# A mixer kernel on one NeuronCore: raw halves of the next pair kept, sums from PSUM copies, GpSimd forming most blocks

## The chip, the cores and the metric

The kernel runs on one core of a Trainium2 chip. What counts is the device time of one execution in microseconds (us). Five engines work at the same time, each through its own instructions in order: TensorE (PE, matrix products; its weight loads are shown as PEld), VectorE (DVE), ScalarE (ACT), GpSimd (POOL) and SyncE (SP, which here only issues DMA transfers). They wait for each other through semaphores. SBUF is the working memory, PSUM the eight banks that TensorE writes its products to, HBM the main memory. GpSimd works on SBUF alone in this kernel.

## The reference

Inputs are float32. Eight batches of 576 tokens pass a windowed attention (8 heads of 64), and then a mixer:

```python
scores = scale * np.matmul(q, k.transpose(0, 1, 3, 2))
mask = (rel >= 0) & (rel < window)
scores = np.where(mask, scores, -1000000000.0)
attn = np.exp(scores - max); attn = attn / (sum + 1e-09)
x = np.matmul(attn, v)                      # 8 x 576 x 512
h = np.maximum(xt @ w_tok1, 0.0) @ w_tok2   # over the tokens, 576 -> 256 -> 576
u = x + h.transpose(0, 2, 1)
h2 = np.maximum(u @ w_ch1, 0.0) @ w_ch2     # over the channels, 512 -> 1536 -> 512
return (u + h2).astype(np.float32)
```

The change concerns the last product over the channels alone. The 8 x 576 tokens are 4,608 columns there.

## The kernel before

**Precision.** Every float32 operand of a large product is kept as two tiles: a high one, a rounded copy that ScalarE makes, and a low one, the difference between the value and its high part. Three matmuls (high x high, low x high, high x low) stand for one product.

**Stages.** Attention and the products over the tokens fill the first 253 us and leave `u` in HBM, as nine chunks of 512 columns (`u_dram`). Then come the channel products. Chunk 0 is done plainly. Chunks 2 and 1 are the *half pair*: the first layer is plain, the second is done on both chunks together with seven products in place of eight (the scheme of Strassen and Winograd on 2 x 2 blocks). Chunks 3 and 4, 5 and 6, 7 and 8 are *pairs*, with seven products in both layers. The seven are called m1 to m7 and run in the order m1, m6, m5, m7, m3, m2, m4 in a pair's first layer.

**The blocks of a pair.** A pair's first layer needs seven combinations of its `u`. With four raw tiles r11, r12, r22, r21 (128 x 512, one quarter of the pair; there are two such sets, t = 0 and t = 1, and the text calls them halves) they are t1 = r12 - r11, r12' = r22 - r12, t2 = r22 - t1 (`sums`, lines 867 to 872) and r11' = r21 - t2 (`sum4`, line 876). `prep` (lines 880 to 888) then forms one half of a block: ScalarE's copy is the high part (line 886), a subtraction on VectorE or GpSimd the low part (line 888). m1 is formed from r11, m6 from t2, m5 from t1, m7 from r12', m3 from r22, m2 from r21, m4 from r11'. r11 and r12 are overwritten by their sums, so m1 has to be formed before `sum4`.

**The half pair's second layer** runs in three groups. Each group has two `mixed_product` calls (first layer, 24 matmuls each) and two `second_product` calls, one for each `ct`. A second product has seven products of six matmuls; each product lands in one of four PSUM banks P, Q, R, S (m1 and m2 share P, m7 and m4 share R, m5 and m3 share S, m6 has Q), and VectorE adds the bank to the output (line 1082) before the next product may use it. After m6, three sums follow: one on VectorE into c22, two on GpSimd into c12 and c21. In the last group the order is m7, m1, m5, m6, m2, m3, m4 for ct = 0 and m7, m5, m1, m6, m3, m2, m4 for ct = 1. The banks of ct = 1 for R and S are the two buffers of the tag `h`.

**What is woven in.** The order on each engine is written by hand: after each product `second_product` calls `after(m)`, and the functions `after0`, `after1`, `tail0` and `tail1` put the work for the first pair's blocks there. In the middle group the raw tiles of half 0 are loaded, GpSimd forms their sums, and m1 and m6 of half 0 are formed. Then half 1 is loaded into the same four tiles, and later half 0 a second time into four other tiles (`homes`), because its raw tiles are gone. In the last group `tail0` forms sums and blocks of half 1, `tail1` those of half 0, both sums on VectorE. m2 and m4 come last, since the tiles that they lie in hold the half pair's weights until its last product.

**After it** `first_product` of the first pair follows on TensorE at once. Its products m1, m6, m5, m7 start the banks P, Q, S, R; VectorE forms x1 (line 1037) from Q and a ScalarE copy of P (line 1034), and x2 (line 1040) from S. m3 adds to S, so it has to wait until x2 has read S.

**Loads.** SyncE issues all of them, in program order. `load_unit` brings the pairs' weights in pieces, two transfers of 896 KB each.

Of the kernel before, what the change touches and what calls it, by code (L numbers as in the profile page):

```python
# [11 lines left out]
F32 = mybir.dt.float32  # L12
# [11 lines left out]
P = 128  # L24
# [71 lines left out]
def mixer_kernel(ctx: ExitStack, tc: tile.TileContext, qh, kh, vh, wt1, wt2, wc1, wc2, out):  # L96
# [493 lines left out]
    with ExitStack() as bctx:  # L590
# [195 lines left out]
        def ended(steps):  # L786
            assert next(steps, None) is None
# [62 lines left out]
        pairs = [(j, j + 1) for j in range(N_PLAIN + N_MIXED, NCHUNK, 2)]  # L850
        comb, raws, pools = {}, {}, {}

        def load_raw(q, t, at=0, homes={}):
            r = raws[at] = {}

            def new(name):
                if name in homes:
                    return homes[name]
                return pools[at].tile([P, CHUNK], F32, name=f"{name}_{q}_{t}", tag=name, bufs=1)

            for name, j, ct in (("r11", 0, t), ("r12", 1, t), ("r22", 1, 2 + t), ("r21", 0, 2 + t)):
                r[name] = new(name)
                nc.sync.dma_start(r[name], u_dram[pairs[q][j]][:, ct])
            for name in ("t1", "t2"):
                r[name] = new(name)

        def sums(t3=True, at=0, eng=nc.vector):
            r = raws[at]
# [131 lines left out]
        def first_product(n, q, f, after, earlier):  # L1000
# [24 lines left out]
            for k, m in enumerate(PRODUCTS):  # L1025
                o = n % NSLOT * SLOT + k * 2 * P
                c = comb[q, m]
                for z, t in enumerate((1, 0) if q == 0 and m in ("m5", "m7", "m3") else (0, 1)):
                    at = slice(o + t * P, o + (t + 1) * P)
                    for y, (w, h) in enumerate(((w1hi, 0), (w1hi, 1), (w1lo, 0))):  # L1030
                        nc.tensor.matmul(b[INTO[m]], w[:, at], c[:, h, t], start=(k < 4 and z == y == 0),  # L1031
                                         stop=(z == 1 and y == 2), skip_group_check=True)
                if m == "m1":
                    nc.scalar.copy(x1, pp)  # L1034
                    next(earlier, None)
                elif m == "m6":
                    nc.vector.tensor_add(x1, qq, x1)
                    next(earlier, None)
                elif m == "m5":
                    nc.vector.tensor_add(x2, ss, x1)  # L1040
                    next(earlier, None)
                elif m == "m7":
                    nc.vector.tensor_add(qq, rr, x2)
                    raw_block("m3", qq)
                elif m == "m3":
                    nc.vector.tensor_add(ss, ss, x1)
                    nc.scalar.activation(g12, ss, AF.Relu)
                    raw_low("m3", qq)
                    positive(t3, qq, g12)
                    sum_block("m7", t3)  # L1050
                elif m == "m2":
                    positive(t1, pp, g12)
                    sum_block("m5", t1)
                    nc.vector.scalar_tensor_tensor(out=t2, in0=qq, scalar=0.0, in1=t1, op0=ALU.max, op1=ALU.add)
                    raw_block("m1", pp)
                    sum_block("m6", t2)
                    raw_low("m1", pp)
                after(m)
# [67 lines left out]
        for g in range(NG):  # L1126
# [14 lines left out]
                    prep(0, {"m3": "m1", "m2": "m6"}[m], 0)  # L1141

            def tail0(m):
                if m == "m6":
                    sums()
                if m in ("m2", "m3"):
                    prep(0, {"m2": "m5", "m3": "m7"}[m], 1, 0, nc.gpsimd)
                if m in ("m3", "m4"):
                    prep(0, {"m3": "m1", "m4": "m6"}[m], 1)
                if m == "m4":  # L1150
                    sum4()

            def tail1(m):
                if m == "m7":
                    prep(0, "m3", 1, 0, nc.gpsimd)
                if m == "m6":
                    sums(True, 1)
                if m in ("m3", "m2", "m4"):
                    prep(0, {"m3": "m5", "m2": "m7", "m4": "m3"}[m], 0, 1, nc.gpsimd)
                if m == "m4":  # L1160
                    sum4(1)

            odd = (3 * g + 1) % 2
            tags = BANKS[odd]
            for i in range(2):
# [3 lines left out]
                if last and i == 0:  # L1169
                    ended(steps)  # L1170
                if last and i == 1:
                    load_unit(0)
                    homes = {name: pg.tile([P, CHUNK], F32, name=f"{name}_x", tag=tag, bufs=1)
                             for name, tag in (("r11", "g12"), ("r12", "t1g"), ("r22", "t2g"), ("r21", "t3g"))}
                    spare = new_tmps(pm, "wt").rearrange("p (n a) c -> p n (a c)", a=2)
                    homes |= {"t1": spare[:, 0], "t2": spare[:, 1]}
                    load_raw(0, 0, 1, homes)
                    load_unit(1)
                    load_unit(2)
            for ct in range(2):  # L1180
                second_product(-1, g, ct, (odd + 1 + ct) % 2, (*slots[ct], 0), (u2c[0], u1[0]), u2[ct],
                               ((after0, after1), (tail0, tail1))[last][ct])
                if g == 1 and ct == 1:
                    load_raw(0, 1)
                load_mixed(2 * g + 2 + ct)
                if not last:
                    store_quarters(2)
        for m, eng in (("m2", nc.vector), ("m4", nc.gpsimd)):
            for t in range(2):
                prep(0, m, t, 1 - t, eng)  # L1190
        mctx.close()
        pools[1] = bctx.enter_context(tc.tile_pool(name="pg2", bufs=1, reuse_waits="tile"))

# [93 lines left out]
```

## Time and profile before

| what | value |
|---|---|
| runs of the kernel | 796.96, 797.24 and 798.72 us, median 797.24 |
| the profiled execution | 798.98 us, of which 797.2 us are the profile's span |
| PE busy | 781.1 us (98%), 5,713 matmul instructions |
| DVE busy | 596.2 us (75%) |
| ACT busy | 403.1 us (51%) |
| POOL busy | 342.3 us (43%) |
| last group of the half pair, ct = 0 | from 420.49 us |
| ct = 1 | from 430.01 us |
| first product of the first pair | from 442.47 us |
| second product of the first pair | from 468.08 us |

Times are from the start of the span. "Busy" counts the time in which an engine had an instruction under way. TensorE's matmuls overlap, so that a matmul of 0.39 us is followed by the next after 0.227 us. A row of the timeline gives start, duration, engine, line, operation, what is written and read, and in brackets the idle time before it with what ended it. A row of the waits gives who waited for whom, and then the total in us, the number of waits and the longest. The granted clock (PEclk) is the share of TensorE's full clock. A tile's name is given without its buffer number: `r` is a raw tile of the first set of four, `r_x` one of the second set, `m` a block, `uf` an output tile, `u_x` the sum that m1 and m6 share, `x` is x1 or x2, `gp` and `op` are PSUM banks of the first and second layer.

### The profile page before, as it was taken

To read this page: it belongs to the slowest core of one execution; us is meant where nothing else is said; L and a number is where in the kernel's file an instruction comes from. 1 tells how busy PE (TensorE), PEld (TensorE's weight loads), DVE (VectorE), ACT (ScalarE), POOL (GpSimd) and SP (SyncE) were. 2 spreads that over 40 slices of the span, in tenths; PEclk is the share of its full clock that TensorE was granted. 3 is DMA by queue.
4 is the path that set the end of the run, shared out by engine and by line. 5 is a ranking of instruction groups with operands and counts; after the bars stand their busy time and mean duration, and the time that the engine had idled before them with its cause. 6 is when DMAs were issued, how large, how long until landed. Compare 5 with 4: busy or idle time off the path is not lost.

```text
span 797.2 us, 15920 instructions
## 1 busy us (share of the span) xinstructions
PE 781.1 (98%) x5713; PEld 650.0 (82%) x5713; DVE 596.2 (75%) x1550; ACT 403.1 (51%) x1149; POOL 342.3 (43%) x298
## 2 busy tenths in 40 slices
PE   8999999999999999999998899999999999999997
PEld 6778888888888888888887688888888888888886
DVE  6998889689884897768888874757766667656576
ACT  6999979989964432463432342325322244324040
POOL 3654445445430001045667540549732638723140
PEclk9999999999999999999999899999999999999999
DMA  9876768767847569895979375765985756955543
GB/s 343 307 235 228 242 221 303 260 212 267 279 138 244 191 207 284 274 298 175 304 229 408 131 290 191 263 239 197 296 322 195 291 184 207 350 211 192 198 163 106
DMA packets 89552, 192.81 MB, mean 242 GB/s; under 512 B 9088, under 2 KB 52864, under 8 KB 87552
## 3 DMA queue, kind: packets, MB, share of 16 engines
q1 hardware_dynamic: 87360, 189.95, 68.9%
q10 hardware_dynamic: 2112, 1.84, 0.7%
q8 instruction: 45, 0.74, 0.4%
q14 instruction: 35, 0.29, 0.1%
HBM read 149.29 MB, written 42.47 MB: 241 GB/s over the span
## 4 chain that ended last, share of the span: by engine, by line
PE 64%; DVE 2%; DMA 2%; issue 1%; ACT 1%; POOL 0%; DVEq 0%; ACTq 0%; POOLq 0%
PE op L1093 22%; PE gp L1031 21%; PE gp L667 12%; PE op L675 4%; DMA u_dram<-u 1%; DMA out<-uf 1%; DVE uf L1082 0%; PE op-1_0_1_3_5769 L1093 0%; PE op-1_1_1_2_6045 L1093 0%; PE op-1_1_1_0_6043 L1093 0%; PE op-1_1_1_3_6046 L1093 0%; PE op-1_0_1_2_5768 L1093 0%; PE op-1_0_0_2_5691 L1093 0%; PE op-1_0_0_3_5692 L1093 0%; PE op-1_0_0_0_5689 L1093 0%
## 5 line engine op out<-in xcount | busy, mean ns | idle before, releaser
L1031 PE MATMUL gp<-m,w1hi 128*128 128x512 f32 x504 | 157.4, 394 | 3.6 <-DVE x L1040 3.6
L1031 PEld LDWEIGHTS gp<-m,w1hi 128*128 128x128 f32 x504 | 95.9, 190 | 24.1 <-DVE x L1040 4.0
L319 ACT ACTIVATE e<-e,nm 128x128 f32<-128x128 f32 x288 | 112.3, 398 | 5.7 <-DVE nm L311 5.6
L1031 PE MATMUL gp<-m,w1lo 128*128 128x512 f32 x252 | 99.0, 393 | 0.0
L1082 DVE TENSOR_TENSOR uf<-op,uf 128x512 f32<-128x512 f32 (+1 forms) x91 | 61.9, 684 | 39.6 <-PE op L1093 31.8
L117 POOL TENSOR_TENSOR m7lo<-t3g,m7hi 128x512 fp32r<-128x512 f32 x18 | 23.4, 1302 | 148.6 <-ACT m7hi L114 148.6
L311 DVE CUSTOM_DVE_ANT_0 e<-s,mask 128x128 f32<-128x128 f32 x288 | 63.5, 286 | 10.4 <-PE s L292 10.4
L232 POOL TENSOR_TENSOR w<-r,c 128x384 f32<-128x384 f32 (+1 forms) x31 | 30.8, 994 | 67.0 <-DVE r L230 56.0
L667 PE MATMUL gp<-ulo,w1hi 128*128 128x512 f32 x144 | 56.1, 390 | 0.2 <-DVE ulo L117 0.2
L319 ACT ACTIVATION_READ_ACCUMULATOR e<-e,nm 128x1 f32 x288 | 56.4, 196 | 0.0
L667 PE MATMUL gp<-uhi,w1hi 128*128 128x512 f32 x144 | 56.1, 390 | 0.0
L1031 PEld LDWEIGHTS gp<-m,w1lo 128*128 128x128 f32 x252 | 47.9, 190 | 10.1
L667 PE MATMUL gp<-uhi,w1lo 128*128 128x512 f32 x144 | 56.0, 389 | 0.0
L117 POOL TENSOR_TENSOR xlo<-x,xhi 128x512 fp32r<-128x512 f32 x32 | 41.1, 1285 | 29.0 <-ACT xhi L114 28.7
L1034 ACT COPY x<-gp 128x512 f32<-128x512 f32 x18 | 10.6, 588 | 75.8 <-PE gp L1031 75.8
L338 PEld LDWEIGHTS xp<-v,pt 128*64 128x64 f32 x1152 | 36.7, 137 | 13.5 <-ACT e L319 9.0
L437 PE MATMUL up<-t2hi,hhi 128*128 128x320 f32 (+1 forms) x128 | 42.9, 335 | 0.0
L326 PE MATMUL pp<-ident,e 128*128 128x128 f32 x288 | 41.5, 278 | 1.4 <-ACT e L319 0.8
L338 PE MATMUL xp<-v,pt 128*64 128x64 f32 x1152 | 41.7, 225 | 1.1 <-ACT pt L328 0.8
L292 PE MATMUL s<-k,q 64*64 64x128 f32 x1152 | 41.6, 278 | 0.9 <-DVE ri L350 0.5
L328 ACT COPY pt<-pp 128x512 f32<-128x512 f32 x72 | 39.0, 587 | 2.4 <-PE pp L326 0.7
L326 PEld LDWEIGHTS pp<-ident,e 128*128 128x128 f32 x288 | 33.1, 141 | 6.7 <-ACT e L319 5.5
(477 smaller groups left out, 2158.7 us busy)
## 6 DMA issues: line engine op xcount, KB each, us to landing
v<-vh SPq DMA_DIRECT2D x36, 512.0 KB, 4.3
w1hi<-w1s SPq DMA_DIRECT2D x18, 896.0 KB, 5.1
w1lo<-w1s SPq DMA_DIRECT2D x18, 896.0 KB, 7.0
w1hi<-w2s SPq DMA_DIRECT2D x18, 896.0 KB, 4.7
w1lo<-w2s SPq DMA_DIRECT2D x18, 896.0 KB, 6.5
raw<-wc SPq DMA_DIRECT2D x32, 384.0 KB, 5.2
q<-qh SPq DMA_DIRECT2D x36, 256.0 KB, 5.0
k<-kh SPq DMA_DIRECT2D x7, 1280.0 KB, 8.3
```

The lines of the kernel that those rows point to most:

```text
L117: eng_lo.tensor_sub(lo, src, hi.bitcast(F32))
L292: nc.tensor.matmul(so, qt[r, j, half], kbs[b][r, n:n + 2, j], start=True, stop=True)
L311: nc.vector.tensor_tensor_reduce(out=e_sb[i, u][:, h], in0=s_ps[i][h // 2 * 2 + u][:, h], in1=mk, scale=-scale, scalar=MAX_F32, op0=ALU.ad ...
L319: nc.scalar.activation(e[:, h], e[:, h], AF.Exp, bias=nm[:, g:g + 1], scale=-1.0, accum_out=sm[:, g:g + 1])
L326: nc.tensor.transpose(pp[:, h], e[:, h], ident)
L328: nc.scalar.copy(pt, pp)
L338: nc.tensor.matmul(xp[half * BLK:(half + 1) * BLK, h], pts[h % 2][:, h // 2, half * BLK:(half + 1) * BLK], vt[:, half, h], start=True, sto ...
L437: nc.tensor.matmul(up[:, :n], hx[:, cs], w[:, tt * S + s0:tt * S + s0 + n], start=False, stop=(k == 6), skip_group_check=True)
L667: nc.tensor.matmul(gp, w[:, w1_at(ft, ct)], x[:, ct], start=(k == 0), stop=(k == 3 * NCT - 1))
L1031: nc.tensor.matmul(b[INTO[m]], w[:, at], c[:, h, t], start=(k < 4 and z == y == 0), stop=(z == 1 and y == 2), skip_group_check=True)
L1082: eng.tensor_add(x, y, x)
L1093: nc.tensor.matmul(bank[:, cols], w[:, o:o + P], x[:, cols], start=(i == 0 and y == 0 and m in ("m1", "m6", "m7", "m5")), stop=(i == 1 and ...
```

## The change

- The raw tiles of half 0, loaded in the middle group, stay in place to the end. The second set of four tiles is loaded with half 1, and the load of half 1 into the first set is gone: four transfers of 256 KB fewer. r11, r12 and r22 of half 1 now come ahead of the first weight piece, r21 behind it.
- The sums of half 1 are formed by `sums_by_psum`: ScalarE copies r12 and r22 into the two buffers of `h` in PSUM, and each of the three subtractions on VectorE takes one operand from there. VectorE forms no sums of half 0 any more, since those of the middle group are kept.
- `tail0` now forms the low parts of m7, m3 and m5 of half 0 on GpSimd, `tail1` those of m1 and m6 of half 1 on VectorE and of m5, m7 and m3 of half 1 on GpSimd. Both `sum4` come at the end of `tail1`.
- In the first pair's first layer, half 0 comes first for all seven products; before, half 1 came first for m5, m7 and m3.

```diff
+        def sums_by_psum(at):
+            r = raws[at]
+            p12, p22 = (ps.tile([P, CHUNK], F32, name=f"{name}_p", tag=tag, bufs=bufs)
+                        for name, (tag, bufs) in zip(("r12", "r22"), BANKS[1][2:]))
+            nc.scalar.copy(p12, r["r12"])
+            nc.scalar.copy(p22, r["r22"])
+            nc.vector.tensor_sub(r["t1"], p12, r["r11"])
+            nc.vector.tensor_sub(r["r12"], r["r22"], p12)
+            nc.vector.tensor_sub(r["t2"], p22, r["t1"])
...
-                for z, t in enumerate((1, 0) if q == 0 and m in ("m5", "m7", "m3") else (0, 1)):
+                for z, t in enumerate((0, 1)):
...
             def tail0(m):
+                if m in ("m7", "m1", "m5"):
+                    prep(0, {"m7": "m7", "m1": "m3", "m5": "m5"}[m], 0, 0, nc.gpsimd)
                 if m == "m6":
-                    sums()
-                if m in ("m2", "m3"):
-                    prep(0, {"m2": "m5", "m3": "m7"}[m], 1, 0, nc.gpsimd)
-                if m in ("m3", "m4"):
-                    prep(0, {"m3": "m1", "m4": "m6"}[m], 1)
+                    sums_by_psum(1)
+
+            def tail1(m):
+                if m in ("m7", "m5"):
+                    prep(0, {"m7": "m1", "m5": "m6"}[m], 1, 1)
+                if m in ("m1", "m6", "m3"):
+                    prep(0, {"m1": "m5", "m6": "m7", "m3": "m3"}[m], 1, 1, nc.gpsimd)
                 if m == "m4":
-                    sum4()
-
-            def tail1(m):
-                if m == "m7":
-                    prep(0, "m3", 1, 0, nc.gpsimd)
-                if m == "m6":
-                    sums(True, 1)
-                if m in ("m3", "m2", "m4"):
-                    prep(0, {"m3": "m5", "m2": "m7", "m4": "m3"}[m], 0, 1, nc.gpsimd)
-                if m == "m4":
-                    sum4(1)
+                    for t in range(2):
+                        sum4(t)
...
                 if last and i == 1:
-                    load_unit(0)
...
-                    load_raw(0, 0, 1, homes)
+                    loads = raw_loads(0, 1, 1, homes)
+                    next(loads)
+                    load_unit(0)
+                    ended(loads)
                     load_unit(1)
                     load_unit(2)
...
-                if g == 1 and ct == 1:
-                    load_raw(0, 1)
...
         for m, eng in (("m2", nc.vector), ("m4", nc.gpsimd)):
             for t in range(2):
-                prep(0, m, t, 1 - t, eng)
+                prep(0, m, t, t, eng)
```

`raw_loads` is the old `load_raw` as a generator that pauses ahead of r21.

**VectorE, from the c22 sum of ct = 0 on.** In the names, `r12_0_1` is r12 of half 1 in the first set of tiles, `r12_x` a tile of the second set, `r12_p` and `r22_p` the PSUM copies, `wt_wt` the tiles of t1 and t2 in the second set, `op-1_2_0_*` and `op-1_2_1_*` the banks of ct = 0 and ct = 1 (0 is P, 1 Q, 2 R, 3 S), `m1_0` the block m1. Before:

```order
L1082 TENSOR_TENSOR uf1_4745<-u2_x_0_5583,uf1_4745 128x512
L869 TENSOR_TENSOR t1_0_1_6140<-r12_0_1_6134,r11_0_1_6132 128x512
L871 TENSOR_TENSOR r12_0_1_6134<-r22_0_1_6136,r12_0_1_6134 128x512
L872 TENSOR_TENSOR t2_0_1_6141<-r22_0_1_6136,t1_0_1_6140 128x512
L1082 TENSOR_TENSOR uf2_5314<-op-1_2_0_0_6267,uf2_5314 128x512
L1082 TENSOR_TENSOR uf1_4745<-op-1_2_0_3_6270,uf1_4745 128x512
L888 TENSOR_TENSOR m1_0_6095<-r11_0_1_6132,m1_0_6095 128x512
L1082 TENSOR_TENSOR uf2_5314<-op-1_2_0_2_6269,uf2_5314 128x512
L888 TENSOR_TENSOR m6_0_6122<-t2_0_1_6141,m6_0_6122 128x512
L876 TENSOR_TENSOR r11_0_1_6132<-r21_0_1_6138,t2_0_1_6141 128x512
L1082 TENSOR_TENSOR uf1_4745<-op-1_2_1_2_6343,uf1_4745 128x512
L1082 TENSOR_TENSOR uf1_4745<-op-1_2_1_3_6344,uf1_4745 128x512
```

And with the change:

```order
L1098 TENSOR_TENSOR uf1_4745<-u2_x_0_5583,uf1_4745 128x512
L879 TENSOR_TENSOR wt_wt_6246<-r12_p_6302,r11_x_6242 128x512
L880 TENSOR_TENSOR r12_x_6243<-r22_x_6244,r12_p_6302 128x512
L881 TENSOR_TENSOR wt_wt_6246<-r22_p_6303,wt_wt_6246 128x512
L1098 TENSOR_TENSOR uf2_5314<-op-1_2_0_0_6257,uf2_5314 128x512
L1098 TENSOR_TENSOR uf1_4745<-op-1_2_0_3_6260,uf1_4745 128x512
L1098 TENSOR_TENSOR uf2_5314<-op-1_2_0_2_6259,uf2_5314 128x512
L1098 TENSOR_TENSOR uf1_4745<-op-1_2_1_2_6335,uf1_4745 128x512
L904 TENSOR_TENSOR m1_0_6095<-r11_x_6242,m1_0_6095 128x512
L1098 TENSOR_TENSOR uf1_4745<-op-1_2_1_3_6336,uf1_4745 128x512
```

Between the c22 sum and the addition of m5 of ct = 1 (the last row of each) stand ten instructions before and eight with the change; six of the ten read SBUF alone, one of the eight does.

**VectorE, behind the last products of ct = 1.** `x1_0_0` and `x2_0_0` are x1 and x2 of the first pair. Before:

```order
L1082 TENSOR_TENSOR uf1_4745<-u2_x_1_5584,uf1_4745 128x512
L869 TENSOR_TENSOR wt_wt_6258<-r12_x_6255,r11_x_6254 128x512
L871 TENSOR_TENSOR r12_x_6255<-r22_x_6256,r12_x_6255 128x512
L872 TENSOR_TENSOR wt_wt_6258<-r22_x_6256,wt_wt_6258 128x512
L1082 TENSOR_TENSOR uf1_4745<-op-1_2_1_3_6344,uf1_4745 128x512
L1082 TENSOR_TENSOR uf2_5314<-op-1_2_1_0_6341,uf2_5314 128x512
L1082 TENSOR_TENSOR uf2_5314<-op-1_2_1_2_6343,uf2_5314 128x512
L876 TENSOR_TENSOR r11_x_6254<-r21_x_6257,wt_wt_6258 128x512
L888 TENSOR_TENSOR m2_0_6414<-r21_x_6257,m2_0_6414 128x512
L888 TENSOR_TENSOR m2_0_6414<-r21_0_1_6138,m2_0_6414 128x512
L1037 TENSOR_TENSOR x1_0_0_6448<-gp0_0_1_6431,x1_0_0_6448 128x512
L1040 TENSOR_TENSOR x2_0_0_6449<-gp0_0_3_6433,x1_0_0_6448 128x512
```

And with the change:

```order
L1098 TENSOR_TENSOR uf1_4745<-u2_x_1_5584,uf1_4745 128x512
L1098 TENSOR_TENSOR uf1_4745<-op-1_2_1_3_6336,uf1_4745 128x512
L1098 TENSOR_TENSOR uf2_5314<-op-1_2_1_0_6333,uf2_5314 128x512
L1098 TENSOR_TENSOR uf2_5314<-op-1_2_1_2_6335,uf2_5314 128x512
L892 TENSOR_TENSOR r11_0_0_5915<-r21_0_0_5921,t2_0_0_5924 128x512
L892 TENSOR_TENSOR r11_x_6242<-r21_x_6245,wt_wt_6246 128x512
L904 TENSOR_TENSOR m2_0_6405<-r21_0_0_5921,m2_0_6405 128x512
L904 TENSOR_TENSOR m2_0_6405<-r21_x_6245,m2_0_6405 128x512
L1053 TENSOR_TENSOR x1_0_0_6439<-gp0_0_1_6422,x1_0_0_6439 128x512
L1056 TENSOR_TENSOR x2_0_0_6440<-gp0_0_3_6424,x1_0_0_6439 128x512
```

The three sums are gone from here; both `sum4` stand behind the last addition of ct = 1, where one of them stood.

**GpSimd, from the half pair's last first-layer block on.** Before:

```order
L117 TENSOR_TENSOR m4lo_x_5_6211<-g1_2_5248,m4hi_x_5_6210 128x512
L1082 TENSOR_TENSOR uf1_4745<-u2_x_0_5583,uf1_4745 128x512
L1082 TENSOR_TENSOR uf2_5314<-u2_x_0_5583,uf2_5314 128x512
L888 TENSOR_TENSOR m5_0_6314<-t1_0_1_6140,m5_0_6314 128x512
L888 TENSOR_TENSOR m7_0_6325<-r12_0_1_6134,m7_0_6325 128x512
L888 TENSOR_TENSOR m3_0_6352<-r22_0_1_6136,m3_0_6352 128x512
L1082 TENSOR_TENSOR uf1_4745<-u2_x_1_5584,uf1_4745 128x512
L1082 TENSOR_TENSOR uf2_5314<-u2_x_1_5584,uf2_5314 128x512
L888 TENSOR_TENSOR m5_0_6314<-wt_wt_6258,m5_0_6314 128x512
L888 TENSOR_TENSOR m7_0_6325<-r12_x_6255,m7_0_6325 128x512
L888 TENSOR_TENSOR m3_0_6352<-r22_x_6256,m3_0_6352 128x512
L888 TENSOR_TENSOR m4_0_6419<-r11_x_6254,m4_0_6419 128x512
```

And with the change:

```order
L117 TENSOR_TENSOR m4lo_x_5_6201<-g1_2_5248,m4hi_x_5_6200 128x512
L904 TENSOR_TENSOR m7_0_6268<-r12_0_0_5917,m7_0_6268 128x512
L904 TENSOR_TENSOR m3_0_6278<-r22_0_0_5919,m3_0_6278 128x512
L904 TENSOR_TENSOR m5_0_6288<-t1_0_0_5923,m5_0_6288 128x512
L1098 TENSOR_TENSOR uf1_4745<-u2_x_0_5583,uf1_4745 128x512
L1098 TENSOR_TENSOR uf2_5314<-u2_x_0_5583,uf2_5314 128x512
L904 TENSOR_TENSOR m5_0_6288<-wt_wt_6246,m5_0_6288 128x512
L1098 TENSOR_TENSOR uf1_4745<-u2_x_1_5584,uf1_4745 128x512
L1098 TENSOR_TENSOR uf2_5314<-u2_x_1_5584,uf2_5314 128x512
L904 TENSOR_TENSOR m7_0_6268<-r12_x_6243,m7_0_6268 128x512
L904 TENSOR_TENSOR m3_0_6278<-r22_x_6244,m3_0_6278 128x512
L904 TENSOR_TENSOR m4_0_6410<-r11_0_0_5915,m4_0_6410 128x512
```

The same number of instructions; three low parts now stand ahead of the two c12 and c21 sums of ct = 0, one between the two pairs of sums, and two (m7 and m3) behind those of ct = 1.

More of the change, by code (lines that the diff above doesn't have):

```diff
@@ L851, in mixer_kernel, with raw_loads @@
         comb, raws, pools = {}, {}, {}
-        def load_raw(q, t, at=0, homes={}):
+        def raw_loads(q, t, at=0, homes={}):
             r = raws[at] = {}
@@ L861, in load_raw @@
             for name, j, ct in (("r11", 0, t), ("r12", 1, t), ("r22", 1, 2 + t), ("r21", 0, 2 + t)):
+                if name == "r21":
+                    yield
                 r[name] = new(name)
@@ L865, in load_raw @@
                 r[name] = new(name)
+        def load_raw(*args):
+            for _ in raw_loads(*args):
+                pass
+        def sums_by_psum(at):
[7 more added lines that the diff above has]
+            nc.vector.tensor_sub(r["t2"], p22, r["t1"])
         def sums(t3=True, at=0, eng=nc.vector):
```

## The prediction

> **What bounds the kernel now.** I read the chain that ended last first, then TensorE's waits.
>
> ```profile
> PE 64%; DVE 2%; DMA 2%; issue 1%; ACT 1%; POOL 0%; DVEq 0%; ACTq 0%; POOLq 0%
> ...
> 451.64 16.60 PE gp L1031 x60
> 468.24 19.11 PE op L1093 x84
> ...
> 773.84 19.24 PE op L1093 x87
> ```
>
> ```profile
> PE gp L1031 <- DVE x L1040: 3.6, 1, 3.6
> PE op-1_2_1_3_6344 L1093 <- DVE uf L1082: 2.6, 1, 2.6
> PE idle L499 <- DVE zero L166: 1.2, 1, 1.2
> ```
>
> From 451.64 us on the chain is TensorE without a gap, so what is won or lost ahead of that moves the end by as much. TensorE's two longest waits of the whole span lie just there: 2.6 us in the half pair's last group (m3 of ct = 1) and 3.6 us in the pair's first product (its m3). The third is at the kernel's start. TensorE's timeline, with rows left out, gives their price:
>
> ```profile
> 430.01 0.39 PE L1093 MATMUL op-1_2_1_2_6343<-m7hi_x,slotb 128*128 128x512 f32 x1
> ...
> 435.23 0.39 PE L1093 MATMUL op-1_2_1_1_6342<-m6hi_x,slotb 128*128 128x512 f32 x1
> 438.22 0.50 PE L1093 MATMUL op-1_2_1_3_6344<-m3hi_x,slotb 128*128 128x512 f32 x1 [2.60 <-DVE uf L1082]
> ...
> 442.47 0.62 PE L1031 MATMUL gp<-m,w1hi 128*128 128x512 f32 x2
> ...
> 447.69 0.39 PE L1031 MATMUL gp<-m,w1lo 128*128 128x512 f32 x1
> 451.64 1.22 PE L1031 MATMUL gp<-m,w1hi 128*128 128x512 f32 x2 [3.57 <-DVE x L1040]
> ...
> 468.08 0.39 PE L1093 MATMUL op<-m6hi,w1hi 128*128 128x512 f32 x1
> ```
>
> Unhindered, matmuls start 0.227 us apart (442.47 to 447.69 is 23 of them), a product of six takes 1.36 us. Against that pace: m3 of ct = 1 starts 2.76 late (438.22 - 435.46); 438.22 to 442.47 is 4.25 for 18 matmuls that take 4.08, 0.17 lost; the pair's m3 starts 3.73 late (451.64 - 447.91); 451.64 to 468.08 is 16.44 for 60 matmuls that take 13.60, 2.84 lost. Together 9.50 us. The last loss is the clock:
>
> ```profile
> 442.50:450.00 7.50, 5.57 (x25) 4.29 (x23) 7.06 (x8) 3.88 (x8) 6.16 (x5) 1.00 0.38 133
> 450.00:451.00 1.00, 0.00 (x0) 0.00 (x0) 0.80 (x2) 0.07 (x1) 1.00 (x2) 0.77 0.00 0
> ...
> 452.00:456.00 4.00, 4.00 (x10) 3.11 (x10) 1.68 (x3) 1.19 (x2) 0.00 (x0) 0.50 0.00 0
> ...
> 457.00:458.00 1.00, 1.00 (x5) 0.81 (x4) 0.69 (x1) 0.41 (x2) 0.55 (x1) 0.82 0.00 0
> ```
>
> In these stretches of the span (PEclk is the third number from the end) it falls to a half at 450.5, inside the long wait, and returns at 457.4. In the shorter wait it stayed:
>
> ```profile
> 435.00:438.00 3.00, 0.61 (x3) 0.19 (x1) 2.90 (x5) 0.00 (x0) 0.61 (x1) 1.00 1.02 423
> ```
>
> Why is VectorE late? Its timeline, and GpSimd's for the same time:
>
> ```profile
> 426.86 0.69 DVE L1082 TENSOR_TENSOR uf<-u_x,uf 128x512 f32<-128x512 f32 x1
> 427.47 1.77 DVE L869 TENSOR_TENSOR t<-r,r 128x512 f32<-128x512 f32 x1
> 429.27 1.68 DVE L871 TENSOR_TENSOR r<-r,r 128x512 f32<-128x512 f32 x1
> 430.87 1.79 DVE L872 TENSOR_TENSOR t<-r,t 128x512 f32<-128x512 f32 x1
> 432.58 0.68 DVE L1082 TENSOR_TENSOR uf<-op-1_2_0_0_6267,uf 128x512 f32<-128x512 f32 x1
> 433.18 0.67 DVE L1082 TENSOR_TENSOR uf<-op-1_2_0_3_6270,uf 128x512 f32<-128x512 f32 x1
> ```
>
> ```profile
> 423.65 1.29 POOL L117 TENSOR_TENSOR m4lo_x<-g,m4hi_x 128x512 fp32r<-128x512 f32 x1 [0.57 <-ACT m4hi_x L114]
> 426.90 3.50 POOL L1082 TENSOR_TENSOR uf<-u_x,uf 128x512 f32<-128x512 f32 x2 [1.96 <-DVE u_x L1082]
> 430.36 1.74 POOL L888 TENSOR_TENSOR m<-t,m 128x512 fp32r<-128x512 f32 x1
> 432.06 3.55 POOL L888 TENSOR_TENSOR m<-r,m 128x512 fp32r<-128x512 f32 x2
> ```
>
> A VectorE instruction on SBUF alone takes 1.7 to 1.8 us while GpSimd works, and GpSimd's 1.75 instead of 1.29: they go by turns, with VectorE's ends (429.24, 430.95, 432.66) 1.71 apart. With an operand in PSUM it takes 0.68 beside a busy GpSimd, and the next starts 0.60 later. So the three sums cost 5.1 us where 1.8 would do, and the addition of m5 of ct = 1, for which TensorE's m3 waits, ends at 438.16:
>
> ```profile
> 437.47 0.69 DVE L1082 TENSOR_TENSOR uf<-op-1_2_1_3_6344,uf 128x512 f32<-128x512 f32 x1
> ...
> 450.10 0.69 DVE L1037 TENSOR_TENSOR x<-gp,x 128x512 f32<-128x512 f32 x1 [0.54 <-ACT x L1034]
> 450.89 0.69 DVE L1040 TENSOR_TENSOR x<-gp,x 128x512 f32<-128x512 f32 x1
> ```
>
> The same sums come again for half 0 in ct = 1, and x2 ends at 451.58.
>
> **The change: ct = 0 and ct = 1.** TensorE's matmuls are the same, and so is all up to 420 us but for four loads. I lay the new order out with the durations above. GpSimd is free at 424.94. Low parts of m7, m3, m5 then take it to 429.2 (1.26 each, and one turn for VectorE's c22 sum, which the same turns delay to 428.0), the c12 and c21 sums to 430.4 and 431.7, m5 of half 1 to 433.0. ScalarE, here and at the end of the group:
>
> ```profile
> 422.95 0.62 ACT L114 CAST m4hi_x<-g 128x512 fp32r<-128x512 f32 x1 [0.81 <-DVE g L926]
> ...
> 449.49 0.58 ACT L1034 COPY x<-gp 128x512 f32<-128x512 f32 x1
> ```
>
> It makes three high parts by 425.6 (the third waits for GpSimd at 424.94) and then the two copies to PSUM. No copy of 512 elements from SBUF to PSUM stands in the trace. The nearest rows are the 0.58 above, out of PSUM, and one group into it:
>
> ```profile
> L202 ACT ACTIVATE a<-raw 128x384 f32<-128x384 f32 x2 | 1.0, 502 | 0.0
> ```
>
> 0.502 for 384 elements gives 0.67 for 512 if all of it scales. I take 0.60 and keep 0.58 to 0.67: the copies end at 426.2 and 426.8, 1.2 us ahead of VectorE at either bound, so that they cost nothing; without that cover each would cost its 0.6. Behind them on ScalarE wait the high parts of half 1, which nobody wants before 432. VectorE's three sums run from 428.0 to 429.8 at 0.60 each. Then the addition of m2 to 430.4, c12 (waits for GpSimd) to 431.2, c21 (the same) to 432.4, m7 of ct = 1 to 433.0, m1's low part to 433.6, m5's addition to **434.2**. TensorE wants it at 435.46: **no wait, 2.76 and 0.17 back**. New is that the copies lie in the banks that ct = 1 writes first: m7 has to wait for the second sum (429.2, wanted at 430.01, 0.8 us to spare), m5 for the third (429.8 against 431.37).
>
> **The change: the end of ct = 1.** Now m3 of ct = 1 starts at 435.46, m4 ends at 439.7, the pair begins at 439.53 and would reach its m3 at 439.53 + 24 x 0.2267 = 444.97. VectorE has the c22 sum at 437.1, and GpSimd its two at 438.2 and 439.5, and goes on with m7, m3 and then m4 twice, whose high parts are ready in time. VectorE adds m4 at 439.76 to 440.4 and has four instructions on SBUF alone: `sum4` twice, m2's low parts twice. GpSimd's m7 runs from 439.6 to 440.75, so the four go by turns with GpSimd's four: the first ends at 440.75 + 0.58 = 441.3, the fourth three turns of 1.71 later at 446.46. x1 to 447.06, x2 to 447.80, and TensorE at **447.86: 2.89 late instead of 3.73, 0.84 back**. Before, the two low parts of m2 ran free (GpSimd was waiting):
>
> ```profile
> 448.28 0.68 DVE L888 TENSOR_TENSOR m<-r_x,m 128x512 fp32r<-128x512 f32 x1
> 448.88 0.68 DVE L888 TENSOR_TENSOR m<-r,m 128x512 fp32r<-128x512 f32 x1
> ```
>
> so two turns more (2.2 us) are spent here against the three sums saved. Bounds: no turns at all, four at 0.60 from 440.4, and x2 is done before 444.97; turns of 1.79 with the first missed by a full GpSimd instruction, 449.2.
>
> **The loads.** Four of 256 KB fewer. SyncE's queue past 418 us, and the landing times from 405 to 470 us:
>
> ```profile
> 418.60 1.00 SPq L694 DMA_DIRECT2D w1s<-wt_wt  x2
> ...
> 420.20 0.42 SPq L847 DMA_DIRECT2D w1lo<-w1s  x1
> ```
>
> ```profile
> r<-u_dram SPq DMA_DIRECT2D x4, 256.0 KB, 3.9
> r_x<-u_dram SPq DMA_DIRECT2D x4, 256.0 KB, 10.4
> ```
>
> r11, r12, r22 go out from 419.7 on, ahead of the 1.8 MB of weights and no longer behind them, so I take 3.9 us: by 424.5. ScalarE wants r12 at 425.6; only past 427.9 does a later landing reach TensorE. The weights leave 1.3 us later and are wanted at 439.5; 20 us cover them. The half order in m5, m7, m3 changes no matmul.
>
> **The clock.** A wait of 2.7 us (2.89 less the pipelined part) remains, between 2.60, where the clock held, and 3.57, where it fell. It fell 2.5 us after the last matmul and was back 6.8 later. In the shorter wait it did not fall though that lasted 2.6, so a fixed delay alone does not explain both; if idle time is summed in stretches of half those 6.8, ending at 450.5, the long wait put 2.46 into one, the shorter 1.28 and 1.32 into two. With a limit of 1.9, in the middle, a wait of 2.7 at a random place passes it in two of three cases (0.2 that it lies whole in one stretch of 3.4, and else 1.6/2.7 that the larger part is over 1.9: 0.2 + 0.8 x 0.59). I take the clock as lost again, for the same 2.84: nothing back. If the boundary falls otherwise, the loss is 1.7 (half of one stretch) to 3.4 (half of two). The Trainium skill ("TensorE: Matmul & The Clock Gate", section "What's actually happening") has the clock halved after at least one idle window of about 3.4 us, the windows running free; read by its letter a wait of 2.7 us is safe. The trace differs in part: it fell after 2.5.
>
> **Sum.** 2.76 + 0.17 + 0.84 = 3.77 back. The profiled execution took 798.98 (span 797.2, 1.78 around it), hence 795.2; it lies 1.74 above the median of 797.24, hence **793.5**.
>
> **Rivals.**
> *A, the clock holds.* The wait of 2.7 is split over two stretches, or too short: 2.84 more, **790.6**. For it: 2.60 passed unharmed. Against: 2.7 is longer, and the place is chance. 0.25. This is also what the skill's rule would give.
> *B, the turns don't meet.* GpSimd's m7 and m3 slip or finish apart from VectorE's four: the wait vanishes, all 9.50 back, **787.7**. Against: in both places in which the two queues were full they took turns without fail. 0.07.
> *C, the sums stay slow or GpSimd is late.* If a PSUM operand does not free the sums, three turns (5.1) replace 1.8, and m7, m5 and m3 of ct = 1 start about 2.1 late in all: **795.6**. Against: 0.68 and 0.67 at 432.58 and 433.18, beside GpSimd. 0.11.
> *D, slower: the raw loads set TensorE's pace.* Load, copy, sum and bank now stand in a row ahead of ct = 1. For each us that r12 lands past 427.9, m7 starts one later and all behind it; past 431.7 the gains in waits are gone. At the 10.4 us of `r_x` before, r12 lands at 430.5: 2.6 lost, 796.1; at 434, 6.1 lost, **799.6**. Against: those loads queued behind the weights. 0.06.
>
> **Chances and range.** Forecast 0.5 (792.6 to 794.8 for its own range: turns 0.3 off, clock loss 1.7 to 3.4), A 0.25, B 0.07, C 0.11, D 0.06, the rest for what I miss. 790.1 to 796.0 holds the forecast, A, C and a part of D. A measurement here can tell 0.2% (1.6 us) from no change. Faster by that is below 795.65: forecast, A, B, half of C, 0.86; same, the rest of C and some of D, 0.09; slower, 0.05.
>
> **What would show it.** Right: no wait at m3 of ct = 1; the three sums at 0.68; one wait at the pair's m3 of about 2.7, released by x2, with `sum4` and m2 at 1.7 beside GpSimd; PEclk at a half for several us after it. Wrong: a wait at m7 of ct = 1 (loads), sums at 1.7 (C), no wait at m3 (B), full clock (A).

## The result and the profile after

| what | before | after the change |
|---|---|---|
| executions compared side by side | 796.96, 797.24, 797.98, 798.72 us | 792.06, 792.17, 792.97, 794.33 us |
| median | 797.61 us | 792.57 us |
| ratio | | 0.9939, 95% interval 0.9919 to 0.9959 |
| profiled execution (span) | 798.98 (797.2) us | 792.06 (790.3) us |
| last group, ct = 0, first matmul | 420.49 us | 419.93 us |
| first pair's second product, first matmul | 468.08 us | 460.98 us |

The change is faster by 0.6%: 5.0 us here, 3.6 in a second comparison below. The forecast was 793.5 us in 790.1 to 796.0.

TensorE's waits in the profile after, longest first (all lines of the code sit 16 further down: L1047 was L1031, L1056 was L1040, L1098 was L1082, L1109 was L1093, L904 was L888, L892 was L876):

```profile
PE gp L1047 <- DVE x L1056: 2.7, 1, 2.7
PE s L292 <- DMA q<-qh: 1.6, 2, 0.9
PE idle L499 <- DVE zero L166: 1.2, 1, 1.2
```

Of the two long waits one is left, at the pair's m3. The other, for `uf` at m3 of ct = 1, is not in the list. TensorE's timeline, rows left out:

```profile
419.93 0.39 PE L1109 MATMUL op-1_2_0_2_6259<-m7hi_x,slothi 128*128 128x512 f32 x1
...
434.67 0.39 PE L1109 MATMUL op-1_2_1_1_6334<-m6hi_x,slotb 128*128 128x512 f32 x1
434.89 0.39 PE L1109 MATMUL op-1_2_1_3_6336<-m3hi_x,slotb 128*128 128x512 f32 x1
...
438.97 0.62 PE L1047 MATMUL gp<-m,w1hi 128*128 128x512 f32 x2
...
447.25 0.73 PE L1047 MATMUL gp<-m,w1hi 128*128 128x512 f32 x2 [2.67 <-DVE x L1056]
...
460.98 0.39 PE L1109 MATMUL op<-m6hi,w1hi 128*128 128x512 f32 x1
```

m3 of ct = 1 starts 0.22 behind the last matmul of m6, the unhindered pace. The pair's m3 should start at 438.97 + 24 x 0.2267 = 444.41 and starts at 447.25, 2.84 late. The 60 matmuls after it take 13.73, against 13.60 unhindered: in this execution the clock held. VectorE's timeline shows why the one wait went and the other stayed:

```profile
427.30 0.68 DVE L879 TENSOR_TENSOR wt_wt<-r_p,r_x 128x512 f32<-128x512 f32 x1
427.90 0.67 DVE L880 TENSOR_TENSOR r_x<-r_x,r_p 128x512 f32<-128x512 f32 x1
428.50 0.68 DVE L881 TENSOR_TENSOR wt_wt<-r_p,wt_wt 128x512 f32<-128x512 f32 x1
...
432.90 0.68 DVE L1098 TENSOR_TENSOR uf<-op-1_2_1_3_6336,uf 128x512 f32<-128x512 f32 x1
...
439.24 0.69 DVE L1098 TENSOR_TENSOR uf<-op-1_2_1_2_6335,uf 128x512 f32<-128x512 f32 x1 [0.27 <-PE op-1_2_1_2_6335 L1109]
439.85 0.87 DVE L892 TENSOR_TENSOR r<-r,t 128x512 f32<-128x512 f32 x1
440.64 1.78 DVE L892 TENSOR_TENSOR r_x<-r_x,wt_wt 128x512 f32<-128x512 f32 x1
442.34 1.78 DVE L904 TENSOR_TENSOR m<-r,m 128x512 fp32r<-128x512 f32 x1
444.04 1.76 DVE L904 TENSOR_TENSOR m<-r_x,m 128x512 fp32r<-128x512 f32 x1
445.72 0.68 DVE L1053 TENSOR_TENSOR x<-gp,x 128x512 f32<-128x512 f32 x1
446.50 0.69 DVE L1056 TENSOR_TENSOR x<-gp,x 128x512 f32<-128x512 f32 x1
```

The three sums with an operand in PSUM (`r_p`) take 0.67 or 0.68 each and start 0.60 apart. The addition of m5 ends at 433.58, before TensorE wants it at 434.89. Of the four instructions on SBUF alone, from 439.85 on, the first takes 0.87 and the others 1.76 to 1.78, beside this GpSimd queue:

```profile
438.87 3.00 POOL L904 TENSOR_TENSOR m<-r_x,m 128x512 fp32r<-128x512 f32 x2
441.83 1.74 POOL L904 TENSOR_TENSOR m<-r,m 128x512 fp32r<-128x512 f32 x1
443.53 1.72 POOL L904 TENSOR_TENSOR m<-r_x,m 128x512 fp32r<-128x512 f32 x1
```

VectorE's ends (440.72, 442.42, 444.12, 445.80) lie 1.70, 1.70 and 1.68 apart: the turns.

### The profile page after: what moved, and what is told of

It is laid out like the page before. It is cut to its first block, busy times and chain, and to the rows that moved or that the text cites. A ratio compares the mean times of both kernels' runs of the same rounds, so it can differ in the third digit from the quotient of the medians.

```text
span 790.3 us, 15910 instructions
## 1 busy us (share of the span) xinstructions
PE 776.4 (98%) x5713; PEld 647.6 (82%) x5713; DVE 591.4 (75%) x1547; ACT 403.8 (51%) x1151; POOL 340.2 (43%) x298
## 4 chain that ended last, share of the span: by engine, by line
PE 66%; DVE 2%; DMA 1%; issue 1%; ACT 0%; POOL 0%; DVEq 0%; POOLq 0%; ACTq 0%
PE op L1109 22%; PE gp L1047 21%; PE gp L667 12%; PE op L675 4%; DMA u_dram<-u 1%; DVE m L904 0%; PE op-1_0_1_3_5769 L1109 0%; PE op-1_1_1_3_6046 L1109 0%; PE op-1_2_1_2_6335 L1109 0%; PE op-1_2_1_0_6333 L1109 0%; PE op-1_2_1_3_6336 L1109 0%; PE op-1_2_0_2_6259 L1109 0%; PE op-1_2_0_3_6260 L1109 0%; PE op-1_2_0_0_6257 L1109 0%; PE op-1_1_1_2_6045 L1109 0%
## 5 line engine op out<-in xcount | busy, mean ns | idle before, releaser
L1047 PE MATMUL gp<-m,w1hi 128*128 128x512 f32 x504 | 155.3, 389 | 2.7 <-DVE x L1056 2.7
L1047 PEld LDWEIGHTS gp<-m,w1hi 128*128 128x128 f32 x504 | 94.5, 188 | 22.7 <-DVE x L1056 3.1
L1047 PE MATMUL gp<-m,w1lo 128*128 128x512 f32 x252 | 98.0, 389 | 0.0
L1098 DVE TENSOR_TENSOR uf<-op,uf 128x512 f32<-128x512 f32 (+1 forms) x91 | 61.9, 683 | 39.7 <-PE op L1109 31.9
L1047 PEld LDWEIGHTS gp<-m,w1lo 128*128 128x128 f32 x252 | 47.3, 188 | 9.8
L437 PE MATMUL up<-t2hi,hlo 128*128 128x320 f32 (+1 forms) x128 | 37.8, 296 | 0.0
```

Source lines behind the costliest of these rows:

```text
L437: nc.tensor.matmul(up[:, :n], hx[:, cs], w[:, tt * S + s0:tt * S + s0 + n], start=False, stop=(k == 6), skip_group_check=True)
L1098: eng.tensor_add(x, y, x)
```

## The experiments

"Clock lost" below is an execution whose mean granted clock was 0.998 or less. (The mean also holds half clock behind the last matmul, which costs nothing. In the traces that is at most 2.25 us, in r7, or 0.0014 of the mean, so that alone it would leave 0.999.) The waits are those of the one profiled execution of each kernel; where an unprofiled execution lost the clock is not on record.

**1. The change again, unaltered (r1).** The question was whether the profiled execution is always longer than the others, as the forecast's 1.74 took it to be, and how often the clock is lost. No edit.

> The changed kernel once more, unaltered, for the spread of its executions. Theory (the clock is lost by chance in the wait of 2.7 us): the executions fall into two kinds, 791.9 to 792.3 us with a mean granted clock of 1.000, and 792.8 to 794.6 with 0.998 to 0.993; the span of each is 1.77 below its time, profiled or not. Rival (the spread comes from the attention stage or from profiling): times vary with the clock at 1.000, or the profiled one stands apart by 1 to 2 us.

Measured: 791.89, 792.8, 794.2, 794.21, 794.93 (the profiled one) and 795.93 us, median 794.2; before, in 13 executions beside it, 797.83; ratio 0.9953 (0.9937 to 0.9969). The clock was lost in four of the six, those of 794.2 and more. Two lie outside what was expected: 792.8 with the clock kept, and 795.93. The windows of this trace, and then those of the trace shown above (columns: window, length, busy time of PE, PEld, DVE, ACT and POOL, granted clock, DMA share, GB/s):

```profile
444.00:447.00 3.00, 0.40 (x2) 0.00 (x0) 2.90 (x3) 0.00 (x0) 1.08 (x1) 1.00 0.01 3
447.00:451.00 4.00, 3.92 (x10) 3.10 (x11) 1.86 (x4) 0.95 (x2) 0.00 (x0) 0.57 0.00 0
451.00:455.00 4.00, 4.00 (x19) 3.27 (x19) 3.37 (x6) 3.03 (x6) 2.29 (x2) 1.00 0.27 58
```

```profile
444.00:447.00 3.00, 0.57 (x3) 0.15 (x1) 2.90 (x4) 0.00 (x0) 1.25 (x1) 1.00 0.02 7
447.00:451.00 4.00, 3.75 (x16) 3.11 (x17) 2.82 (x6) 1.20 (x2) 0.00 (x0) 1.00 0.00 0
```

The same kernel with the same wait (2.7 in both lists of waits): once TensorE's clock is 0.57 on average in the 4 us that follow and ten matmuls start in them, once it is full and sixteen start. With the first comparison there are ten executions of the change. Four kept the clock (791.89, 792.06, 792.17, 792.8; mean 792.2), six lost it (792.97 to 795.93; mean 794.4). The difference, 2.2 us, is what one loss costs here on average. This trace has a second delay that the other has not, 1.03 us at a later second product, waiting for VectorE's `uf`, so its own time is not the clock alone. The 60 matmuls behind the wait give the price of this one loss: 15.34 us (447.07 to 462.41) against 13.60 unhindered.

**2. r21 from PSUM too (r2).** If the turns with GpSimd are the whole of the remaining wait, it must go when the four instructions at the end of ct = 1 read one operand from PSUM. ScalarE copies r21 of both halves into two banks that are idle then.

```diff
-            eng.tensor_sub(r["r11"], r["r21"], r["t2"])
+            eng.tensor_sub(r["r11"], r.get("r21p", r["r21"]), r["t2"])
+
+        def r21_to_psum(at, bank):
+            r = raws[at]
+            r["r21p"] = ps.tile([P, CHUNK], F32, name=f"r21p_{at}", tag=bank, bufs=1)
+            nc.scalar.copy(r["r21p"], r["r21"])
...
-                eng.tensor_sub(c[:, 1, t], raws[at][SOURCE[m]], c[:, 0, t].bitcast(F32))
+                r = raws[at]
+                eng.tensor_sub(c[:, 1, t], r.get("r21p", r["r21"]) if m == "m2" else r[SOURCE[m]],
+                               c[:, 0, t].bitcast(F32))
...
+                if m in ("m6", "m2"):
+                    r21_to_psum(*{"m6": (0, "up"), "m2": (1, "av")}[m])
```

> As the change, but ScalarE also copies r21 of both halves into two free PSUM banks during ct = 1, and both sum4 and both low parts of m2 on VectorE take r21 from there, so that none of the four reads SBUF alone. Theory (the wait that is left at the pair's m3 is four turns with GpSimd): the four take 0.60 each, x2 ends at about 444.3 where TensorE wants it at 444.6, the wait of 2.67 us and the clock loss go, 789.0 to 789.4 us in every execution, clock 1.000. Rival (VectorE is late because of how much stands behind ct = 1, or because it waits for ScalarE's high parts): 2 us or more of the wait stay, 791 us or more.

Measured: 788.59, 788.74, 789.06 and 789.38 us, median 788.9; ratio to before 0.9889 (0.9876 to 0.9903). No execution lost the clock. VectorE at the same place, then TensorE's start of the pair, of its m3 and of its second product:

```profile
438.61 0.69 DVE L1105 TENSOR_TENSOR uf<-op-1_2_1_2_6335,uf 128x512 f32<-128x512 f32 x1 [0.26 <-PE op-1_2_1_2_6335 L1116]
439.21 0.68 DVE L892 TENSOR_TENSOR r<-r21p,t 128x512 f32<-128x512 f32 x1
439.81 0.68 DVE L892 TENSOR_TENSOR r_x<-r21p,wt_wt 128x512 f32<-128x512 f32 x1
440.41 1.28 DVE L910 TENSOR_TENSOR m<-r21p,m 128x512 fp32r<-128x512 f32 x2
441.67 0.69 DVE L1060 TENSOR_TENSOR x<-gp,x 128x512 f32<-128x512 f32 x1
```

```profile
438.34 0.62 PE L1054 MATMUL gp<-m,w1hi 128*128 128x512 f32 x2
...
443.78 0.62 PE L1054 MATMUL gp<-m,w1hi 128*128 128x512 f32 x2
...
457.38 0.39 PE L1116 MATMUL op<-m6hi,w1hi 128*128 128x512 f32 x1
```

The times lie up to 0.4 below what was expected. Four instructions in 2.5 us instead of 5.9, and m3 starts 5.44 after the pair's first matmul, 24 x 0.2267, without a wait. From the first matmul of ct = 0 (419.30) to the second product is 38.08 us, which is 168 x 0.2267 to the hundredth: nothing is lost in this stretch any more. The turns were the whole wait. This version beats both kernels, by 3.3 us the change's executions that kept the clock and by 5.5 those that lost it.

**3 and 4. The clock alone (r3, r4).** If the slow matmuls after the wait come from TensorE's idleness in it, matmuls that do nothing useful, put into the wait, must bring their time back and leave the rest. In r3 the kernel before gets 14 extra matmuls ahead of m3 of the pair's first product, into a PSUM bank that nobody reads; in r4 the change gets 10.

```diff
                 c = comb[q, m]
+                if n == 0 and m == "m3":
+                    fill = ps.tile([P, CHUNK], F32, name="fill", tag="up", bufs=1)
+                    for _ in range(14):
+                        nc.tensor.matmul(fill, w1hi[:, :P], comb[q, "m1"][:, 0, 0], start=True, stop=True)
```

> The kernel before, with 14 extra matmuls (3.2 us of TensorE work, into a bank that nobody reads) between m7 and m3 of the pair's first product, where TensorE waits 3.7 us; their result is not used. Theory (2.84 us of the profiled execution was clock loss, which varies from one execution to the next, and profiling itself costs nothing): clock 1.000 in all, 795.9 to 796.4 us, hardly any spread, m3 at 451.6 in its trace as before. Rival (the clock loss is 2.84 in every execution, and profiling adds 1.74): median 794.4 with the profiled one at 796.1. Second rival (the slow matmuls after the wait have another cause than idleness): no gain.

> The change, with 10 extra matmuls (2.27 us, into a bank that nobody reads) at the same place. Theory: the wait for x2 stays where it is, the clock is full in every execution, 791.8 to 792.4 us with no execution above 792.6. Rival (the spread of the changed kernel has another source): executions up to 794 us as before.

Measured: r3 794.52 to 796.26 us in eight executions, median 795.2, ratio 0.9971 (0.9961 to 0.9982), 2.6 below the kernel before. r4 791.36 to 792.54 in six, median 791.94, ratio 0.9927 (0.9916 to 0.9939), clock kept in all. TensorE in r3, and in r4:

```profile
446.75 3.33 PE L1031 MATMUL fill<-m,w1hi 128*128 128x512 f32 x14
450.51 0.73 PE L1035 MATMUL gp<-m,w1hi 128*128 128x512 f32 x2 [0.43 <-DVE x L1044]
```

```profile
444.75 2.43 PE L1047 MATMUL fill<-m,w1hi 128*128 128x512 f32 x10
447.60 0.74 PE L1051 MATMUL gp<-m,w1hi 128*128 128x512 f32 x2 [0.42 <-DVE x L1060]
```

r3 is faster than was expected (795.9 to 796.4), and the clock was expected to be kept in every execution. m3 comes as late as without the extra matmuls: 31.13 us after the first matmul of ct = 0 in r3 (419.38 to 450.51), 31.15 before; 27.33 in r4 (420.27 to 447.60), 27.32 after the change. What is gained is gained behind it. So the price of the idleness is separate from that of the lateness: 2.6 us before, and in the change 2.5 (794.4 - 791.94) in the executions that lost the clock, nothing much (792.2 - 791.94) in those that did not. In r3 the 2.6 us wait of m3 of ct = 1 is still there and the clock was lost in two of eight executions all the same. No trace shows where, but no other wait of r3's list is above 1.2, so a wait of 2.6 alone seems not to be safe. The profiled execution of r3 took 795.12, amid its other seven: being profiled adds nothing that could be seen.

**5 and 6. One half of the change at a time (r5, r6).** r5 is the change with the sums of half 1 read from SBUF; r6 is the kernel before with the PSUM copies in its first set of sums and no raw half kept.

```diff
                 if m == "m6":
-                    sums_by_psum(1)
+                    sums(True, 1)
```

```diff
+        def sums_by_psum(at):
...
                 if m == "m6":
-                    sums()
+                    sums_by_psum(0)
```

> The change with the three sums of half 1 on SBUF operands again (no copies to PSUM): the kept raw half alone. Theory (an operand in PSUM takes VectorE out of the turns with GpSimd): the sums take 1.7 us each, a wait of 1.3 to 1.8 us comes back at m3 of ct = 1, the wait at the pair's m3 grows to 3.5 to 3.9 us, the clock is lost in nearly all executions; 796.0 to 797.3 us. Rival (what matters is that VectorE forms half as many sums, not where they read): within 0.5 us of the change, 793.6.

> The kernel before with its first three sums (half 1, in ct = 0) taken from PSUM copies in the same way, and nothing else: the PSUM copies alone. Theory: the sums take 0.68, the wait at m3 of ct = 1 falls from 2.6 to about 1.1 us, the one at the pair's m3 stays at 3.5 to 3.8 with the clock lost; 795.7 to 796.6 us, 1.6 less than before. Rival (the PSUM copies do all that the change does): 793 to 794 us. Second rival (the copies cost ScalarE or TensorE more than they bring): no gain.

Measured: r5 median 796.76 us, ratio 0.9991 (0.998 to 1.0002), not to be told from before (797.57 in the executions beside it); r6 median 796.1, ratio 0.9984 (0.997 to 0.9998). The clock was lost in ten of ten and nine of ten executions. TensorE's waits and two of VectorE's rows, r5 first:

```profile
PE gp L1047 <- DVE x L1056: 4.0, 1, 4.0
PE op-1_2_1_3_6332 L1109 <- DVE uf L1098: 1.3, 1, 1.3
```

```profile
426.81 1.78 DVE L885 TENSOR_TENSOR wt_wt<-r_x 128x512 f32<-128x512 f32 x1
428.62 1.66 DVE L887 TENSOR_TENSOR r_x<-r_x 128x512 f32<-128x512 f32 x1
```

```profile
PE gp L1041 <- DVE x L1050: 3.6, 1, 3.6
PE op-1_2_1_3_6348 L1103 <- DVE uf L1092: 1.0, 1, 1.0
```

```profile
426.49 0.68 DVE L873 TENSOR_TENSOR t<-r_p,r 128x512 f32<-128x512 f32 x1
...
429.49 1.31 DVE L898 TENSOR_TENSOR m<-r,m 128x512 fp32r<-128x512 f32 x1
...
432.42 1.77 DVE L886 TENSOR_TENSOR r<-r,t 128x512 f32<-128x512 f32 x1
```

Without the copies the sums take turns as before, and 1.3 of the wait at m3 of ct = 1 stays. Counted from the first matmul of ct = 0, the pair begins 1.56 us later than in the change (20.60 against 19.04) and x2 ends 2.84 later (30.10 against 27.26), so the wait for x2 grows from 2.7 to 4.0. With the copies alone the sums are quick, but VectorE still forms m1's and m6's low parts and a `sum4` there (the second fence of r6), and the sums of half 0 again in ct = 1. Alone the two parts bring 0.8 (not clear of noise) and 1.5 us, 2.3 together; the change brings 4.0 (797.6 to 793.58, the medians over all executions of before and of the change). Each part leaves a wait that the other would have taken away.

**7. The raw loads behind the weights (r7).** Rival D held that a late r12 or r22 would set TensorE's pace. Here the first weight piece is sent ahead of the raw tiles again.

```diff
-                    loads = raw_loads(0, 1, 1, homes)
-                    next(loads)
                     load_unit(0)
-                    ended(loads)
+                    load_raw(0, 1, 1, homes)
```

> The change with the raw tiles of half 1 loaded behind the first weight piece (two transfers of 896 KB), as before, and not ahead of it. Theory (load, copy, sum and bank stand in a row ahead of ct = 1): r12 and r22 land at about 429 to 431 instead of 426, ScalarE waits for them, TensorE waits 1 to 3 us at m7 of ct = 1 for VectorE's second sum, and the time grows by that, 794.5 to 797 us. Rival (the loads have time to spare in either place): no new wait, within 0.5 us of the change.

Measured: 792.79 to 798.01 us in nine executions, median 795.19, ratio 0.9968 (0.9953 to 0.9984); the clock lost in seven. Landing times from 405 to 470 us, of the change and of r7, then the copy to PSUM that kept ScalarE waiting (r22 in the change, r12 in r7, where TensorE's m7 of ct = 1 follows in the same fence):

```profile
r_x<-u_dram SPq DMA_DIRECT2D x4, 256.0 KB, 5.6
```

```profile
r_x<-u_dram SPq DMA_DIRECT2D x4, 256.0 KB, 8.3
```

```profile
426.45 0.59 ACT L878 COPY r_p<-r_x 128x512 f32<-128x512 f32 x1 [1.00 <-DMA r_x<-u_dram]
```

```profile
427.93 0.59 ACT L877 COPY r_p<-r_x 128x512 f32<-128x512 f32 x1 [3.89 <-DMA r_x<-u_dram]
429.90 0.50 PE L1109 MATMUL op-1_2_1_2_6335<-m7hi_x,slotb 128*128 128x512 f32 x1 [1.29 <-DVE r_x L880]
```

The raw tiles land 2.7 us later in the median, the first copy starts 3.06 later (424.87 in the change, 427.93 here), and m7 of ct = 1 waits 1.29 for the second sum, released at the place that the rival named. TensorE reaches the pair's m3 28.89 us after the first matmul of ct = 0 (418.93 to 447.82) instead of 27.32, 1.57 later, and the median over all executions is 1.6 above the change's 793.58. The mechanism is real; in the change itself it has no effect, though ScalarE waited 1.00 there.

## Why the prediction was right, and where it was off

The mechanism of both waits was right, and their sizes too. That the total came within 1 us is partly luck: 2.84 us was charged for a clock loss that the traces price at 1.74 to 2.84 and that came in six of ten executions, and 1.74 was taken off for an offset that r1 and r3 do not show. The two offset each other.

**Wait at m3 of ct = 1, 2.76 + 0.17 back: right.** The sums were forecast at 0.60 each from 428.0 to 429.8, and ran from 427.30 to 429.18; the addition of m5 was forecast to end at 434.2, and ended at 433.58. This execution reached ct = 0 at 419.93 instead of 420.49, 0.56 earlier, which accounts for most of both differences.

**End of ct = 1, 2.89 late: right.** Measured 2.84, a wait of 2.67 against 2.7, released by x2, with the four instructions in turns. r2 shows that the turns are its cause. From the first matmul of ct = 0 to the pair's m3 the kernel before took 31.15 and the change 27.32: **3.83 back, where 3.77 was forecast.**

**Copies on ScalarE: right.** 0.58 and 0.59 in place of the estimated 0.60.

**Loads, 3.9 us: too short by about 2.** The three transfers were issued from 418.94 to 420.39, and r22's copy was released at 426.45, 6.1 after the last of the three issues ended. The step that failed is that they were costed like the four `r` loads of the kernel before (issued from 413.34 on); the landing of the four here was 5.6 in the median. Two weight transfers of 896 KB stood behind those loads too (at 415.30), so what made these slower is open. The forecast's cover, 0.8 us at m7 and 1.2 on ScalarE, took it up: r22's copy ended at 427.04, and the third sum, which reads it, started at 428.50 without a wait.

**The clock, "lost again": what it did in six of ten.** "Two of three cases" was the right size, and so was the choice of the likelier case. But a single time was forecast for something that goes one way or the other from execution to execution, and a median of few of them lands on either side: 792.57 in the first comparison, 794.2 in the second. The argument with summed idle time in stretches of 3.4 us, which the prediction inferred from two waits, is borne out by all nine traces (the table in the last section): the stretches are there, and the limit of 1.9 lies where the traces put it, between 1.86 and 2.14. Of the rule of the Trainium skill ("TensorE: Matmul & The Clock Gate", section "What's actually happening"), by the letter of which 2.7 us is safe, the free-running windows of about 3.4 us agree with the traces. That a whole window has to be idle does not: in r7 2.31 us of idle time in one stretch were enough.

**The 1.74 between the profiled time and the median: this step was wrong.** It was taken off as if the profiled execution were always that much longer. r1 and r3 show their profiled executions amid the rest. 798.98 lies within the spread of the executions of the kernel before, 795.82 to 799.11 in the 13 beside r1. The traces of all kernels differ in how long the clock stays halved (6.8 us in the one of before, 3.4 in the four others that lost it) and in when ct = 0 starts (418.9 to 420.5). Without that step the forecast would have been 795.2 for an execution that loses the clock, where the six had a mean of 794.4, and rival A 798.98 - 3.77 - 2.84 = 792.4, where the four that kept it had 792.2. As printed, 790.6, A was 1.6 too low. The 0.8 by which the forecast was too high fits a shorter loss in some of the six: the 2.84 came from a trace with 6.8 us of half clock, while r1's, with 3.4, lost 1.74. The mean clocks suggest both kinds among the six, 0.997 and 0.998 in two, but 0.994 and 0.995 in three, which is more than one stretch (0.0021 of the mean) and the end (at most 0.0014) take together. That is an inference; only one execution of the change that lost the clock has a trace.

**The rivals.** A happened in four of ten executions. B did not happen (r2 shows what it would have given: 788.9, where 787.7 was forecast). C did not happen, and r5 shows slow sums on the chip: 796.76, where 795.6 was forecast. D did not happen, and r7 shows its mechanism.

## What to carry to other kernels

Where VectorE and GpSimd both work on SBUF tiles, count the turns: each VectorE instruction with both operands in SBUF took 1.1 us more here, and one operand copied to an idle PSUM bank by an idle ScalarE (0.59 us) brought it from 1.7 back to 0.6. Price a TensorE wait as two things, its length and the loss of the clock behind it, and give the second a chance and not a yes or no, from the length of the wait and the stretches below; matmuls that do nothing useful, put into the wait, separate the two and bring the second back. Never carry the offset of one profiled execution into a forecast without knowing where it comes from.

## What the runs showed of the hardware that was not expected

**A wait of 2.6 to 2.7 us loses the clock or not by where it falls.** Executions that lost it, by the waits of the kernel:

| kernel | waits here, us | clock lost |
|---|---|---|
| before (beside r1 to r7) | 2.6 and 3.6 | 36 of 36 |
| r5 | 1.3 and 4.0 | 10 of 10 |
| r6 | 1.0 and 3.6 | 9 of 10 |
| r7 | 1.3 and 2.7 | 7 of 9 |
| the change | 2.7 | 6 of 10 |
| r3 | 2.6 (and 0.43 after the extra matmuls) | 2 of 8 |
| r2, r4 | 0.4 or less | 0 of 10 |

Of before, one execution of 4383 us, far outside all others, is left out of this table.

The traces record when the granted clock changes, and in all nine it does so only on a grid of 3.41 us. Half clock lasted one such stretch (r1: 447.31 to 450.73; r5, r6 and r7 alike) or two (before: 450.53 to 457.36), and every length of full clock between two changes, from 338 to 788 us, is a whole multiple of it. The grid lies elsewhere in each execution. TensorE's idle time (3.41 less its busy time by the profile) in single stretches of the grid:

| trace | stretch from, us | idle in it, us | clock behind it |
|---|---|---|---|
| before, wait of 3.6 | 447.12 | 2.46 | half |
| before, wait of 2.6 | 433.47 and 436.88 | 1.27 and 1.34 | full |
| the change | 442.09 and 445.50 | 0.93 and 1.75 | full |
| r1 (the same kernel) | 443.90 | 2.67 | half |
| r7, wait of 2.7 | 445.51 | 2.31 | half |
| r7, at the end | 786.84 | 2.14 | half |
| r3, at the end | 787.64 | 1.86 | full |

In no stretch of the nine traces is the idle time between 1.86 and 2.14; wherever it is 2.14 or more the clock is halved behind it, and wherever it is 1.86 or less at full clock it stays full. So the same wait of 2.67 kept the clock when the grid cut it in two and lost it when it lay in one stretch. From these figures comes an estimate, with a limit between 1.86 and 2.14 for the larger of the two parts: a wait of 2.67 at a random place loses the clock in 53 to 69 of 100 cases (6 of 10 did), one under 1.86 with no other idle time near it never, one over 4.28 always. The price falls on the work after the wait. One stretch at half cost 1.74 to 1.76 us over the 60 matmuls (r1, r5, r6, r7); in before, where the clock fell 1.1 us before TensorE resumed and stayed at half for a second stretch, it cost 2.84.

**Transfers of the same 256 KB landed after 3.9, 5.6, 8.3 or 10.4 us**, each the median of four. It was 3.9 for half 1 into the first set of tiles in the kernel before, 5.6 in the change ahead of and between the weights, 8.3 in r7, where the one difference from the change is that a weight piece goes ahead, and 10.4 for the second set in the kernel before, also behind one weight piece. r7 shows that the place in the queue matters; what else sets 10.4 against 8.3, and 3.9 against 5.6, no run shows.

**The turns are strict.** Against a full GpSimd queue VectorE's two-operand SBUF instructions end 1.66 to 1.71 apart (before, the change, r5 and r6), and a PSUM operand freed every one of the seven that were moved. The Trainium skill ("SBUF — State Buffer", section "SBUF: two separate sides") describes the port pair that the two engines share as an exclusive lock that an instruction holds to its end; these ends agree, and the 0.68 beside a busy GpSimd does too, since the lock is stated for two SBUF inputs.
